# Attention and SwiGLU on one core: two VectorE casts one slot later, and V of batch 2 issued earlier in chunk 0

## The chip, the cores and the metric

The kernel runs on 1 core of one Trainium2 chip. The metric is the device time of one execution in microseconds (us). Engines are named as in the profile: PE is TensorE, DVE is VectorE, ACT is ScalarE, POOL is GpSimd, SP is SyncE.

## The reference

An attention with a learned decay for 8 batches, 8 heads, 576 positions and a head size of 64, followed by a feed-forward layer over 4608 tokens of width 512 with an inner width of 1536:

```python
def _attn_ref(q, k, v, s):
    scores = scale * np.matmul(q, k.transpose(0, 1, 3, 2))
    cum = np.cumsum(np.maximum(s, 0.0), axis=-1)
    bias = -(cum[:, :, :, None] - cum[:, :, None, :])
    scores = np.where(causal, -1000000000.0, scores + np.minimum(bias, 0.0))
    ...  # softmax over the last axis
    return np.matmul(attn, v)

def _moe_ref(x, w_gate, w_val, w_out, rms_g):
    xn = x / np.sqrt(np.mean(x * x, axis=-1, keepdims=True) + 1e-06) * rms_g
    g = xn @ w_gate
    silu = g * (1.0 / (1.0 + np.exp(-g)))
    return silu * (xn @ w_val) @ w_out
```

## The kernel before

**Stages.** A prologue does most of batch 0's attention. Then nine chunks of 512 tokens go through the feed-forward layer (`ffn`, line 660), and the attention of the later batches is threaded between their matmuls. A chunk has 12 blocks `fb` of the inner width: four matmuls give the gate (line 670, a bank of the PSUM ring `psF` of four), ACT takes a tanh of it into `T` (673), four more matmuls give the value (679, another bank of `psF`), DVE forms `U` from `T` and the gate's bank (682) and, one block later, `Ht` from `U` and the value's bank (675). Then come four output groups `tb` of 12 matmuls with `wout_sb` (692), whose results ACT copies (697) and SP stores.

**Slots.** Between the groups of matmuls `step` (line 599) is called, 36 times a chunk; each call is one slot, and the number of the slot in the chunk is its phase. In chunk 0 slot 2fb+1 follows the gate of block fb and slot 2fb+2 its value; slots 25 to 36 lie in the output groups, three to a group. A slot first emits what the slot before it left over (`pending`: the second half of the exponentials and the causal mask of a score step), then the scaling of finished attention rows, at most one entry of each side queue (`act_side`, `v_side`, `pool_side`, `dve_side`), and then a score step, an attention-times-V step or a transposition. An entry of a side queue is a pair of a condition and an action, and only the head of a queue is looked at. `later(queue, lag, fns)` gives a condition of a number of slots from now; `early` does too, and also asks for a phase below 24. The engines execute what is emitted for them strictly in that order: an instruction that waits holds all that is behind it on its engine.

**Batch 1's Q and K** are loaded by SP in the prologue as 32-bit numbers into `kq32` and cast to bf16 into `kqn` (`cast`, line 135): K's four full row groups by ACT and POOL, Q's groups 0 and 1 by DVE in slots 3 and 4 (the line that the diff changes), groups 2 and 3 by POOL in slots 3 and 4. PE then transposes `kqn` (line 184, into `psT` or a bank of `psF`), and ACT or DVE copies the result to `kqT` (190, 192). Behind the casts in `dve_side` stands `check(0, (0,))`: three instructions on batch 0's K (`check_mag`, line 369, and two `check_max`, 375), one in each odd slot.

**V** of a batch is loaded in five DMAs issued by POOL (`load_v`, line 173; the instruction is at 175), each casting to bf16 on the way, through `v_side`, one in an odd slot. After the last attention step of batch 0, in slot 10, `after_av` queues V of batch 2 with a lag of 16. `step` leaves the V queue and the POOL queue alone in slots 30 to 33 of chunk 0 and the V queue also from slot 34 on. So two of batch 2's V loads are issued in slots 27 and 29 of chunk 0 and three in chunk 1.

**Batch 2's Q and K** are loaded by ACT from slot 14 on; POOL casts Q in slots 24 to 28 (149, and 141 for the last rows) and K from slot 34 on (141).

**Attention rows** of a block (b, qb) of 128 positions: after the second half of the heads ACT or DVE sums the squares (321, 325), POOL forms the factor `al_all` in two instructions (328, 331), DVE scales the rows into `xs_sb` (338), and they get into `xnT` by a transposing DMA of SP (348) or, for batch 0 and block (1,3), by PE (357) and a copy. Chunk 1 needs batch 1's rows up to and including block (1,3); (1,3) is transposed by PE in slot 34 of chunk 0, between two output groups.

Of the kernel before, what the change touches and what calls it, by code (L numbers as in the profile page):

```python
# [26 lines left out]
def kernel(  # L27
# [107 lines left out]
    def cast(eng, b, w, r0, r1, h0=0, h1=H):  # L135
        o = kqn[:, b % 2, w, r0:r1, h0:h1, :]
        i = kq32[:, w].rearrange("p h (r d) -> p r h d", d=D)[:, r0:r1, h0:h1, :]
        if eng is nc.scalar:
            eng.activation(out=o, in_=i, func=AF.Copy)
        else:  # L140
            eng.tensor_copy(out=o, in_=i)  # L141
# [17 lines left out]
    def kq_dma(b, w, c):  # L159

        if w == 0:
            n = rows(c)
            src = kqn[0:n, b % 2, 0, c].rearrange("p h d -> p (h d)")
            dst = kqTx[:, b % 2, 0, c, :, 0:n]
        elif c < 4:
            src = kqn[32 * c:32 * c + 32, b % 2, w, 0:4].rearrange("p r h d -> p (r h d)")
            dst = kqTx[:, b % 2, w, c].rearrange("d h (r p) -> d (h r) p", r=4)
        else:
            src = kqn[0:64, b % 2, w, 4].rearrange("p h d -> p (h d)")
            dst = kqTx[:, b % 2, w, 4, :, 0:64]  # L170
        nc.sync.dma_start_transpose(out=dst, in_=src)

    def load_v(b, c):
        n = rows(c)
        nc.gpsimd.dma_start(  # L175
            out=v_sb[0:n, b % 2, c, :, 0:64],
            in_=v[b, :, c * 128:c * 128 + n, :].rearrange("h p d -> p h d"))
# [157 lines left out]
    def x_scale(b, qb):  # L335
        n = rows(qb)
        col = b * NSC + qb
        nc.vector.scalar_tensor_tensor(  # L338
            out=xs_sb[0:n, (b * NSC + qb) % NX, :], in0=x_sb[0:n, (b * NSC + qb) % NX, :],
            scalar=al_all[0:n, col:col + 1], in1=g_row[0:n], op0=ALU.mult, op1=ALU.mult)  # L340

    def xt_dma(b, qb):

        n = rows(qb)
        t0 = (b * S + qb * 128) % RING
        m = min(n, RING - t0)
        i = (b * NSC + qb) % NX
        nc.sync.dma_start_transpose(out=xnT[:, :, t0:t0 + m], in_=xs_sb[0:m, i, :])
        if m < n:
            nc.sync.dma_start_transpose(out=xnT[:, :, 0:n - m], in_=xs_sb[m:n, i, :])  # L350
# [30 lines left out]
    slot = [0]  # L381
    first, chunk = [0], [0]
# [11 lines left out]
    pool_side, dve_side, v_side, act_side = [], [], [], []  # L394
# [5 lines left out]
    def ready(lag, *key):  # L400
        return at(*key) + lag <= slot[0]

    def run_side(queue):
        if queue and queue[0][0]():
            queue.pop(0)[1]()
            return True
        return False

    def later(queue, lag, fns):
        t = slot[0] + lag  # L410
        queue.extend((lambda: slot[0] >= t, f) for f in fns)
# [17 lines left out]
    def phase():  # L429

        return slot[0] - first[0]
# [14 lines left out]
    def casts(b):  # L446

        def key(c):  # L450
            load_k(b, c)
            done["K", b, c] = slot[0]
            if c == NSC - 1:
                check(b)

        def over(w):
            done["cast", b, w] = slot[0]
            if b + 1 < B and (w == 1 or b + 1 < KB):
                loads(b + 1, w, early, 4)
            if w == 1:  # L460
                x_seq.extend((b, ww, c) for c in range(NSC) for ww in ((1, 0) if b >= KB else (1,)))
            else:
                done["cast", b] = slot[0]
                check(b)

        def free(w):
            return ready(0, "check", b - 2, w) and (
                ready(0, "T", b - 2) if w == 0 and b < KB + 2 else
                b < XB + 2 or ready(4, "X", b - 2, w, 4))
        if b >= KB:  # L470
            pool_side.extend((lambda: free(0) and slot[0] % 2 == 0, lambda c=c: key(c)) for c in range(NSC))
        fns = [(1, lambda r=r: cast_x(nc.gpsimd, b, 1, r)) for r in range(NSC)]
        fns += [(1, lambda: over(1))]
        if b < KB:
            fns += [(0, lambda r=r: cast(nc.gpsimd, b, 0, r, r + 1)) for r in range(NSC)]
            fns += [(0, lambda: over(0))]
        pool_side.extend((lambda w=w: ready(7, "raw", b, w) and free(w), f) for w, f in fns)
# [4 lines left out]

    def after_av(b):
        if b + 2 < B:
            (early if b else later)(v_side, 6 if b else 16, [
                lambda r=r: load_v(b + 2, r) for r in range(NSC)]
                + [lambda: done.__setitem__(("V", b + 2), slot[0])])

# [15 lines left out]
    def do_s(key, pair=None):  # L504
        b, kb, g = key
        second = s_step(b, kb, g, pair)
        done["S", b, kb, g] = slot[0]
        if kb == 4:
            done["S", b, 4, 1] = slot[0]
        last["S"] = slot[0]  # L510
        return second
# [12 lines left out]
    def do_xt(key, pX=None):  # L524
        b, qb = key
        xt_step(b, qb, pX)
        done["XT", b, qb] = slot[0]
        last["T"] = slot[0]
# [13 lines left out]
    def can_s():  # L542
        if not s_seq or not slot_free():
            return False
        b, kb, g = s_seq[0]
        if b == 1 and (phase() < 24 and phase() % 2 == 0 or kb == 4 and at("AV", 1, 3, 1) > slot[0]):
            return False
        due = SLOTS * ((b * S + kb * 128) // DM) - (26 if b == 1 else 18 if b < 4 else 14)
        if slot[0] - last["S"] < (4 if slot[0] < due - 24 else 3 if slot[0] < due else 2):
            return False  # L550
        if b >= XB:
            return all(ready(5, "X", b, 1, c) for c in (kb, min(kb + 1, 4))) and (
                ready(5, "X", b, 0, kb) if b >= KB else ready(3, "T", b) if kb >= 3 else
                all(ready(3, "T", b, hp, 0) for hp in (2 * g, 2 * g + 1)))
        if kb >= 3 and not ready(3, "T", b):
            return False
        if kb == 4:
            return True
        return all(ready(3, "T", b, 2 * g + j, w) for j in (0, 1) for w in (0, 1))
# [18 lines left out]
    def by_pe(b, qb):  # L578

        return b == 0 or (b, qb) == (1, 3)  # L580
# [18 lines left out]
    def step(bare=False):  # L599

        slot[0] += 1
        while pending:
            pending.pop(0)()
        moved = False
        if scaled[0] < len(x_list):
            b, qb = x_list[scaled[0]]
            if ready(3, "AV", b, qb, 1):
                x_scale(b, qb)
                scaled[0] += 1
                if not by_pe(b, qb):  # L610
                    assert xt_seq[0] == (b, qb)
                    xt_dma(*xt_seq.pop(0))
                    done["XT", b, qb] = slot[0] + 4
                    moved = True
        run_side(act_side)

        if not moved and x_seq and slot[0] - last["X"] >= 2 and not (
                scaled[0] < len(x_list) and ready(1, "AV", *x_list[scaled[0]], 1)):
            b, w, c = x_seq[0]
            if (ready(2, "cast", b, 1) and ready(1, "S", b - 2, 4, 0)  # L620
                    and (w == 1 or ready(7, "K", b, c))):
                x_seq.pop(0)
                kq_dma(b, w, c)
                done["X", b, w, c] = last["X"] = slot[0]
                if b >= KB and (w, c) == (0, NSC - 1) and b + 2 < B:
                    casts(b + 2)
        bare = bare or chunk[0] == 0 and 30 <= phase() <= 33
        if slot[0] % 2 and not bare and not (chunk[0] == 0 and phase() >= 34):
            run_side(v_side)
        if not bare:  # L630
            run_side(pool_side)
        run_side(dve_side)
        if can_s():
            pending.append(do_s(s_seq.pop(0)))
            if t_seq and t_seq[0][0] == 1 and can_t():
                do_t(t_seq.pop(0))
            return
        n = 0
        if can_xt():
            do_xt(xt_seq.pop(0))  # L640
            n += 1
        if can_av():
            do_av(av_seq.pop(0))
            n += 1
        if n < 2 and t_seq and can_t():
            do_t(t_seq.pop(0))
# [133 lines left out]
    with tc.manual_schedule():  # L780
# [26 lines left out]
        ACT, DVE, POOL = nc.scalar, nc.vector, nc.gpsimd  # L807
# [89 lines left out]
        def done_cast(w):  # L897
# [4 lines left out]
            lambda: (cast(POOL, 1, 0, 2, 3), cast(POOL, 1, 0, 3, 4)),  # L902
            lambda: (cast(POOL, 1, 1, 2, 3), done_cast(0)),
            lambda: cast(POOL, 1, 1, 3, 4), lambda: done_cast(1), lambda: cast(POOL, 1, 1, 4, 5)])
        later(dve_side, 3, [lambda r=r: cast(DVE, 1, 1, r, r + 1) for r in (0, 1)])
        later(v_side, 0, [
            lambda: load_v(1, 0), lambda: load_v(1, 1), lambda: load_v(1, 2),
            lambda: nc.gpsimd.dma_start(out=wout_sb,
# [204 lines left out]
```

## Time and profile before

| | us |
|---|---|
| median of 3 runs | 373.54 |
| runs | 373.54, 372.38, 373.56 |
| the profiled execution | 373.4 |
| its span, first to last instruction | 371.5 |
| PE busy in it | 346.3 (93%) |
| chunk 0's first gate matmul | 30.83 |
| chunk 1's first gate matmul | 74.53 |

The span is the time from the first to the last instruction on the core; 1.9 us of the execution's time lie outside it. A row of a view in order of time gives start, duration, engine, line, operation, output and inputs, count, and in brackets how long the engine stood idle before it and what ended that. Rows of consecutive instructions of one kind are merged into one with their count. The ends of matmuls are modelled, so rows of PE overlap at their edges.

### The profile page before, as it was taken

The numbers are of one execution on the slowest core, as the hardware profiler recorded it, in microseconds if no ns is written. First come the engines' busy times: TensorE is split into PE (matmuls) and PEld (weight loads), VectorE is DVE, ScalarE is ACT, GpSimd is POOL, SyncE is SP. The second block draws the span as 40 slices with busy tenths as digits, with TensorE's granted clock in tenths as the row PEclk, the third lists the DMA queues.
The fourth block names the chain that finished last, engine by engine and source line by source line (L and its number), as shares of the span: only waits on it lengthen the run. The fifth ranks groups of instructions, "written<-read, shape, count | busy, mean of one in ns | idle before, by whom it ended". The sixth has DMA issues, their size and how long they took to land.

```text
span 371.5 us, 6891 instructions
## 1 busy us (share of the span) xinstructions
PE 346.3 (93%) x2312; PEld 162.7 (44%) x2356; DVE 277.1 (75%) x523; ACT 238.7 (64%) x624; POOL 176.4 (47%) x281
## 2 busy tenths in 40 slices
PE   1888999899999999899999999999999999999992
PEld 1553444354444444444444444444444444444441
DVE  6777989499887878788889888885488558827820
ACT  3977687457977597777768776776777644223311
POOL 5968625966757474778837934533222300000000
PEclk9999999999999999999999999999999999999998
DMA  7999999999949499959969974993300230020011
GB/s 231 169 229 233 178 230 193 155 210 209 182 113 120 44 210 126 175 61 212 149 167 206 157 105 118 112 103 53 106 16 15 44 106 3 0 85 30 0 61 62
DMA packets 125627, 46.23 MB, mean 124 GB/s; under 512 B 104912, under 2 KB 120784, under 8 KB 125584
## 3 DMA queue, kind: packets, MB, share of 16 engines
q0 software_dynamic: 59920, 11.80, 42.9%
q1 hardware_dynamic: 53040, 24.33, 32.5%
q10 hardware_dynamic: 12624, 9.59, 10.4%
q8 instruction: 20, 0.33, 0.4%
q14 instruction: 23, 0.19, 0.2%
HBM read 38.16 MB, written 9.44 MB: 128 GB/s over the span
## 4 chain that ended last, share of the span: by engine, by line
PE 61%; DVE 14%; POOL 8%; issue 6%; DMA 5%; ACT 4%; ACTq 0%; POOLq 0%; DVEq 0%
PE psF L692 19%; PE psF L670 17%; PE psF L679 17%; PE psS L250 3%; DVE U L682 3%; DMA kq<-in_q_dram 3%; DVE Ht L675 2%; DVE x_sb L315 2%; POOL v_sb L175 2%; DVE xs_sb L338 2%; ACT E L274 2%; DVE acc L375 2%; POOL E L283 2%; DMA kq<-in_k_dram 1%; POOL kqn L141 1%
## 5 line engine op out<-in xcount | busy, mean ns | idle before, releaser
L274 ACT ACTIVATE E<-psS,biasK 128x256 bf16<-128x256 f32 (+3 forms) x352 | 115.1, 416 | 19.1 <-PE psS L250 18.0
L670 PE MATMUL psF<-xnT,wg_sb 128*128 128x512 bf16 x426 | 110.3, 379 | 2.6 <-DVE Ht L675 0.9
L679 PE MATMUL psF<-xnT,wv_sb 128*128 128x512 bf16 x408 | 109.3, 380 | 1.4
L692 PE MATMUL psF<-wout_sb,Ht 128*128 128x512 bf16 x419 | 100.5, 379 | 0.5 <-issue 0.2
L682 DVE SCALAR_TENSOR_TENSOR U<-T,psF 128x512 bf16<-128x512 f32 x108 | 73.7, 682 | 29.2 <-ACT T L673 29.0
L283 POOL TENSOR_SCALAR_AFFINE_SELECT E<-E 128x512 bf16<-128x512 bf16 x72 | 51.5, 716 | 85.5 <-ACT E L274 85.1
L673 ACT ACTIVATE T<-psF 128x512 f32<-128x512 f32 x108 | 64.6, 598 | 42.8 <-PE psF L670 37.5
L675 DVE TENSOR_TENSOR Ht<-U,psF 128x512 bf16<-128x512 bf16 x99 | 67.7, 683 | 6.6
L670 PEld LDWEIGHTS <-wg_sb 128*128 128x128 bf16 x432 | 38.8, 98 | 47.1 <-issue 8.0
L679 PEld LDWEIGHTS <-wv_sb 128*128 128x128 bf16 x432 | 38.6, 98 | 42.6 <-issue 4.6
L692 PEld LDWEIGHTS <-Ht 128*128 128x128 bf16 x432 | 38.7, 98 | 42.0 <-issue 2.3
L338 DVE SCALAR_TENSOR_TENSOR xs_sb<-x_sb,al_all,g_row 128x512 bf16<-128x512 bf16 (+1 forms) x40 | 31.9, 800 | 16.4 <-POOL al_all L331 14.8
L697 ACT ACTIVATE osb<-psF 128x512 f32<-128x512 f32 x36 | 21.4, 595 | 33.5 <-PE psF L692 30.5
L321 ACT ACTIVATE xs_sb<-x_sb 128x512 bf16<-128x512 bf16 (+1 forms) x36 | 23.0, 641 | 22.3 <-DVE x_sb L315 22.0
L175 POOL DMA_DIRECT2D v_sb<-in_v_dram x40 | 35.5, 888 | 0.3 <-issue 0.2
L375 DVE TENSOR_TENSOR acc<-acc,mag 128x1280 bf16<-128x1280 bf16 x32 | 29.0, 922 | 0.4
L250 PE MATMUL psS<-kqT 64*128 64x256 bf16 (+2 forms) x304 | 26.8, 262 | 1.7 <-ACT E L274 1.1
L306 PEld LDWEIGHTS <-E 128*128 128x128 bf16 x320 | 23.1, 101 | 11.3 <-POOL E L283 0.8
L328 POOL TENSOR_SCALAR al_all<-ss_all 128x1 f32<-128x1 f32 (+1 forms) x40 | 11.1, 278 | 29.8 <-ACT xs_sb L321 24.0
L300 PEld LDWEIGHTS <-E 128*128 128x128 bf16 x256 | 21.2, 101 | 8.1 <-DVE x_sb L315 0.7
L331 POOL TENSOR_TENSOR al_all<-al_all,mhalf 128x1 f32<-128x1 f32 (+1 forms) x40 | 22.3, 557 | 3.3
L141 POOL CAST kqn<-kq 128x512 bf16<-128x512 f32 (+1 forms) x30 | 20.7, 710 | 5.8 <-DMA kq<-in_k_dram 3.7
(94 smaller groups left out, 271.9 us busy)
## 6 DMA issues: line engine op xcount, KB each, us to landing
out_dram<-osb SPq DMA_DIRECT2D x36, 256.0 KB, 2.2
kq<-in_q_dram ACTq DMA_DIRECT2D x6, 1024.0 KB, 6.7
v_sb<-in_v_dram POOLq DMA_DIRECT2D x32, 128.0 KB, 6.0
kq<-in_k_dram ACTq DMA_DIRECT2D x2, 1024.0 KB, 9.3
kqn<-in_k_dram POOLq DMA_DIRECT2D x16, 128.0 KB, 4.8
wg_sb<-in_moe_w_gate_dram POOLq DMA_DIRECT2D x2, 768.0 KB, 10.1
wv_sb<-in_moe_w_val_dram POOLq DMA_DIRECT2D x2, 768.0 KB, 12.5
wout_sb<-in_moe_w_out_dram POOLq DMA_DIRECT2D x1, 1536.0 KB, 14.7
```

Source lines behind the costliest of these rows:

```text
L175: nc.gpsimd.dma_start(out=v_sb[0:n, b % 2, c, :, 0:64], in_=v[b, :, c * 128:c * 128 + n, :].rearrange("h p d -> p h d"))
L250: nc.tensor.matmul(pair[par][:, j * W:j * W + M], lhsT=kT, rhs=qT, start=(j == 0), stop=(j == nj - 1))
L274: nc.scalar.activation(out=eo, in_=ei, func=AF.Exp, scale=0.125, bias=biasK[:, kb, bh:bh + 1])
L283: nc.gpsimd.affine_select(out=Ev[:, :, 0:nq], in_=Ev[:, :, 0:nq], pattern=[[0, nh], [1, nq]], compare_op=ALU.is_ge, fill=0.0, base=0, chan ...
L338: nc.vector.scalar_tensor_tensor(out=xs_sb[0:n, (b * NSC + qb) % NX, :], in0=x_sb[0:n, (b * NSC + qb) % NX, :], scalar=al_all[0:n, col:col ...
L375: nc.vector.tensor_tensor(out=acc[:, sl], in0=acc[:, sl], in1=mag[:, sl], op=ALU.max)
L670: nc.tensor.matmul(Gp, lhsT=wg_sb[:, cc, fs], rhs=xnT[:, cc, x0:x0 + DM], start=(cc == 0), stop=(cc == CC - 1))
L673: nc.scalar.activation(out=T, in_=Gp, func=AF.Tanh, scale=0.5)
L675: nc.vector.tensor_tensor(out=Ht[:, fb - 1, :], in0=pend[0], in1=pend[1], op=ALU.mult)
L679: nc.tensor.matmul(Vp, lhsT=wv_sb[:, cc, fs], rhs=xnT[:, cc, x0:x0 + DM], start=(cc == 0), stop=(cc == CC - 1))
L682: nc.vector.scalar_tensor_tensor(out=U, in0=T, scalar=1.0, in1=Gp, op0=ALU.add, op1=ALU.mult)
L692: nc.tensor.matmul(Op, lhsT=Ht[:, fb, tb * 128:(tb + 1) * 128], rhs=wout_sb[:, fb, :], start=(fb == 0), stop=(fb == FB - 1))
```

## The change

The lag of the entry for DVE's two casts of batch 1's Q goes from 3 to 4 slots. The lag of batch 2's V goes from 16 to 10, and the phase from which chunk 0 issues no V goes from 34 to 24, so that its first two loads come in slots 21 and 23 and the other three, as before, in chunk 1. The entries behind the casts in `dve_side` move with them: the check of batch 0's K from slots 5, 7 and 9 to 7, 9 and 11.

```diff
     def after_av(b):
         if b + 2 < B:
-            (early if b else later)(v_side, 6 if b else 16, [
+            (early if b else later)(v_side, 6 if b else 10, [
                 lambda r=r: load_v(b + 2, r) for r in range(NSC)]
                 + [lambda: done.__setitem__(("V", b + 2), slot[0])])
...
-        if slot[0] % 2 and not bare and not (chunk[0] == 0 and phase() >= 34):
+        if slot[0] % 2 and not bare and not (chunk[0] == 0 and phase() >= 24):
             run_side(v_side)
...
-        later(dve_side, 3, [lambda r=r: cast(DVE, 1, 1, r, r + 1) for r in (0, 1)])
+        later(dve_side, 4, [lambda r=r: cast(DVE, 1, 1, r, r + 1) for r in (0, 1)])
```

## The prediction

> **What bounds the kernel now.** I read the page's busy shares first, then busy time by stretches, then the chain of waits, then single engines' rows in order of time around the places where the change acts.
>
> ```profile
> span 371.5 us, 6891 instructions
> PE 346.3 (93%) x2312; PEld 162.7 (44%) x2356; DVE 277.1 (75%) x523; ACT 238.7 (64%) x624; POOL 176.4 (47%) x281
> ```
>
> TensorE (PE) is busy for 93% of the span: a change pays only where it takes away one of the few stretches in which PE stands still, and any microsecond that PE gets back early moves all that is queued behind it. The busy time by stretches (columns: stretch, its length, then busy time and instruction count of each engine) finds two of them in chunk 0, which ends with the last of these stretches:
>
> ```profile
> 36.00:42.00 6.00, 4.98 (x41) 2.79 (x41) 5.86 (x11) 3.56 (x7) 5.01 (x6) 1.00 1.32 201
> 42.00:48.00 6.00, 5.95 (x53) 3.12 (x53) 5.93 (x13) 4.61 (x12) 3.05 (x6) 1.00 1.53 163
> ...
> 66.00:74.50 8.50, 6.93 (x54) 3.31 (x54) 3.48 (x7) 3.98 (x14) 8.16 (x14) 1.00 0.90 141
> ```
>
> From 36 to 42 us PE is idle for 6.00 - 4.98 = 1.02 us while VectorE (DVE, third) is full. From 66 to 74.5 us PE is idle for 8.50 - 6.93 = 1.57 us while GpSimd (POOL, fifth) is full. Between, at 42 to 48, PE has nothing to gain. The first edit acts in the first place, the V edits in the second.
>
> **Edit 1, DVE's two casts of batch 1's Q one slot later.** They stood at slots 3 and 4 and go to 4 and 5. DVE, ACT, PE and POOL in order of time (start, duration, idle time before in brackets):
>
> ```profile
> 35.39 0.43 DVE L141 CAST kqn<-kq 128x512 bf16<-128x512 f32 x1 [1.39 <-DMA kq<-in_q_dram]
> 35.73 0.68 DVE L682 SCALAR_TENSOR_TENSOR U<-T,psF 128x512 bf16<-128x512 f32 x1
> 36.33 0.85 DVE L141 CAST kqn<-kq 128x512 bf16<-128x512 f32 x1
> 37.11 0.67 DVE L675 TENSOR_TENSOR Ht<-U,psF 128x512 bf16<-128x512 bf16 x1
> ```
> ```profile
> 33.62 0.60 ACT L673 ACTIVATE T<-psF 128x512 f32<-128x512 f32 x1
> ```
> ```profile
> 37.83 1.02 PE L670 MATMUL psF<-xnT,wg_sb 128*128 128x512 bf16 x4 [0.88 <-DVE Ht L675]
> 38.69 0.39 PE L184 MATMUL psT<-ident_bf,kqn 128*128 128x128 bf16 x4
> ```
> ```profile
> 36.86 0.79 POOL L141 CAST kqn<-kq 128x512 bf16<-128x512 f32 x1
> ```
>
> The cast of slot 3 stands on DVE ahead of the gate product U of block 1 (L682), and waits 1.39 us for the 1 MB transfer of Q, which lands at 35.39. U's input T was ready at 33.62 + 0.60 = 34.22, so U is held 35.73 - 34.22 = 1.51 us by a cast that it doesn't need. Behind U stand the second cast and Ht of block 1 (L675), and it is this Ht that PE waits for, 0.88 us, before it may fill that psF bank with block 3's gate.
>
> With the casts one slot later DVE's order is U, cast, Ht, cast. U runs in the idle time before the transfer lands (34.2 to 34.9); the first cast still starts at 35.39; Ht follows it at 35.39 + 0.43 = 35.8 and ends by 36.5 in place of 37.11 + 0.67 = 37.78. PE comes to that point at 37.83 - 0.88 = 36.95, so the 0.88 us goes whole. What is late next: the transposition of Q at 38.69 reads all four casts. One PE group (38.69 - 37.83 = 0.86) after 36.95 is 37.81; GpSimd's own cast ends at 36.86 + 0.79 = 37.65, and DVE's second cast, now behind Ht, starts at 36.4 and ends by 37.3 at its slower price of 0.85. So both are just in time, and no new wait is larger than 0.1 us.
>
> DVE stays full afterwards, so what does it allow PE to keep? Its total work until 45 us is the same, but one U (0.60 from start to start, 36.33 - 35.73) has left the queue behind the transfer.
>
> ```profile
> 45.50 0.68 DVE L190 COPY kqT<-psT 128x512 bf16<-128x512 bf16 x1
> ```
>
> This copy out of psT, in slot 12, comes 0.6 us earlier, at 44.9. The lower bound of the edit is thus 0.60 us (DVE's gain), the upper bound 1.02 (all of PE's idle time in the stretch). Since 42 to 48 us shows no PE wait although DVE was late all through it, PE's needs there have slack, and I take 1.0, near the upper end. The three check instructions of batch 0's K move two slots later (to 7, 9 and 11), as one queue runs one entry a slot; they take the place of nothing on PE and cost nothing while that slack holds; if it is gone, up to the difference of the bounds, 0.4.
>
> The two casts differ: 0.43 where DVE started first, 0.85 beside a GpSimd instruction. The Trainium skill, SBUF — State Buffer, section "Who interferes with whom", says that a VectorE cast in a two-port mode and a GpSimd instruction shut each other out for the whole instruction, and the one that starts first wins; the 0.85 agrees. By that rule the second cast, still next to GpSimd's cast at 36.86, makes one of the two end about 0.4 later (an estimate from that page's rule and the rows), and the edit would be worth 0.6.
>
> **Edit 2, V of batch 2 at slots 21 and 23, none after slot 24 of chunk 0.** Before, two of the five loads were issued at slots 27 and 29. The chain of waits in order of time (start, length):
>
> ```profile
> 66.28 0.90 POOL v_sb L175
> ...
> 68.72 0.56 POOL al_all L331
> 69.28 0.91 POOL v_sb L175
> ...
> 70.53 0.58 POOL al_all L331
> 71.14 1.15 DVE xs_sb L338
> ...
> 72.33 0.40 PE psT L357 x4
> ```
>
> PE waits for the scaled rows of block (1,3), which need their factor al_all, and that stands on POOL behind both V loads, 0.90 + 0.91 = 1.81 us of issuing. Three rows say how much of this comes back:
>
> ```profile
> 68.28 0.19 ACT L321 ACTIVATION_READ_ACCUMULATOR xs_sb<-x_sb 128x1 f32 x1
> ```
> ```profile
> 69.32 0.75 DVE L338 SCALAR_TENSOR_TENSOR xs_sb<-x_sb,al_all,g_row 128x512 bf16<-128x512 bf16 x1 [1.60 <-ACT E L274]
> ```
> ```profile
> 68.05 2.76 PE L692 MATMUL psF<-wout_sb,Ht 128*128 128x512 bf16 x12
> ```
>
> The sum of squares of (1,3) is ready at 68.28 + 0.19 = 68.47. POOL's chain may move up by 1.81, from 70.53 + 0.58 = 71.11 to 69.3; the input allows the same to within 0.1. The scaling takes 0.75 (row at 69.32) instead of 1.15 (beside GpSimd's casts of K), so it ends at about 70.1, before PE comes free at 68.05 + 2.76 = 70.81. The wait of 72.33 - 70.81 = 1.52 us then goes whole, with 0.7 to spare. With edit 1's 1.0 us PE, DVE, ACT and POOL are all earlier alike, and the spare stays.
>
> At their new place the loads cost POOL the same 1.81 us:
>
> ```profile
> 57.88 0.56 POOL L331 TENSOR_TENSOR al_all<-al_all,mhalf 128x1 f32<-128x1 f32 x1
> 58.79 0.64 POOL L283 TENSOR_SCALAR_AFFINE_SELECT E<-E 128x512 bf16<-128x512 bf16 x1 [0.34 <-ACT E L274]
> 61.19 0.64 POOL L283 TENSOR_SCALAR_AFFINE_SELECT E<-E 128x512 bf16<-128x512 bf16 x1 [1.77 <-ACT E L274]
> 61.78 0.61 POOL L149 CAST kqn<-kq 128x512 bf16<-128x512 f32 x1
> 63.29 0.19 POOL L328 TENSOR_SCALAR al_all<-ss_all 128x1 f32<-128x1 f32 x1 [0.90 <-DVE rZ L313]
> ```
>
> POOL is free for 0.34 us before 58.79, 1.77 before 61.19 and 0.90 before 63.29, 3.01 in all. The load of slot 21 starts at 58.4 and pushes the mask of 58.79 to 59.3; that of slot 23 runs from about 60.0 to 60.9, before the mask of 61.19. So it costs nothing downstream. If that cover were gone, at most the 1.81 would come back to the last third.
>
> What is late next there is block (1,2)'s transfer into xnT, which chunk 1's first matmul needs. Its issue, its time to landing and the matmul:
>
> ```profile
> 70.09 1.19 SPq L348 DMA_TRANSPOSE xnT<-xs_sb  x1
> ```
> ```profile
> xnT<-xs_sb SPq DMA_TRANSPOSE x1, 3.4
> ```
> ```profile
> 74.53 1.03 PE L670 MATMUL psF<-xnT,wg_sb 128*128 128x512 bf16 x4
> ```
>
> It lands at 70.09 + 3.4 = 73.5, 1.0 us before it is used. It moves up only by one load, 0.9, and the matmul by 1.52, so 0.4 us of slack is left; the slack falls but isn't used up.
>
> **Sum.** 1.0 + 1.52 = 2.5 us. The profiled execution took 373.4 us, 1.9 around its span of 371.5; it becomes 370.9. The median of the three runs shown, 373.54, is 0.14 above it: 371.0. After 74.5 us nothing of the change is left but the earlier start, the remaining three V loads keep their slots, and PE is the bound, so I let the gain stand to the end. By the skill's rule for the casts it would be 371.4.
>
> **Rivals.** *One of the two waits stays.* Edit 1: DVE's full queue puts the wait back elsewhere, and only 1.5 comes: 372.0. For it speaks DVE at 5.86 and 5.93 of 6.00 us; against it, PE's full 5.95 beside the second. Edit 2: block (1,2)'s transfer takes its place at chunk 1's start because it lands later than 3.4, and only 1.0 comes: 372.5. For it speaks the 0.4 us of slack; against it, that the V loads' own traffic has left that stretch.
>
> *Nothing comes*, since a later wait on something that does not move (a transfer) takes both back: 373.5. Against it: 93% busy PE, and the loads behind chunk 0 are issued from the queues that move.
>
> *Slower.* The queue of GpSimd's transfers is long at the new place, and an issue may hold POOL until what is ahead of it has landed:
>
> ```profile
> v_sb<-in_v_dram POOLq DMA_DIRECT2D x1, 64.0 KB, 15.6
> ```
> ```profile
> 45.85 0.74 POOL L175 DMA_DIRECT2D v_sb<-in_v_dram  x1
> ```
> ```profile
> v_sb<-in_v_dram POOLq DMA_DIRECT2D x1, 128.0 KB, 3.7
> ```
>
> The last V load of batch 1, issued at 45.85, lands at 61.5. Were slot 21's load held until then and slot 23's until that one has landed, 3.7 later and 0.9 for its issue, POOL would be at 66.1, then a mask (0.64) and a cast (0.61), and the factor of 63.29 would come at 67.4: 4.1 late, less 1.81, is 2.3 lost on the chain that PE waits for: 375.8. It decides from the point at which that factor comes after 63.29 + 1.81 = 65.1. Against it: the issue at 45.85 took 0.74 with the queue as full.
>
> *The change does not do what it says*: the loads miss slots 21 and 23 and go to chunk 1. They are off the last third all the same: 371.0 too.
>
> **How the numbers follow.** Full gain 0.60 (its own range 370.2 to 371.6, from 0.6 to 1.02 for edit 1 and half a microsecond of changed overlaps either way); one wait stays 0.20, of it 0.12 at 372.0 and 0.08 at 372.5; nothing comes 0.08; slower 0.10; misses its slots 0.02. Measurement tells about 0.3%, 1.1 us: faster means below 372.4. Faster 0.60 + 0.12 + 0.02 = 0.74, same 0.08 + 0.08 = 0.16, slower 0.10. The range 370.2 to 372.6 takes in the first two cases and leaves out less than 2 in 10.
>
> **What would show it.** Right: U of block 1 starts near 34.2 before a cast that still waits for Q's transfer; no 0.88 before block 3's gate; two V loads on POOL between 58 and 61 us and none between 64 and 70; no wait of PE for the scaled rows at the end of chunk 0; chunk 1's first gate near 72.0 instead of 74.53. Wrong: a transposition of Q that waits for a cast, PE idle at 42 to 48 us, a V issue of several microseconds, or chunk 1 starting early and the last instruction not.

## The result, and the profile after

| kernel | median, us | runs | against the kernel before |
|---|---|---|---|
| before | 373.35 | 6 (372.38 to 373.56) | |
| changed | 370.10 | 6 (369.39 to 371.13) | ratio 0.9925, 95% interval 0.9909 to 0.9942 |
| changed, second comparison | 369.89 | 6 (369.16 to 370.59) | 0.9900 (0.9868 to 0.9932), before 373.01 |
| changed, third comparison | 370.85 | 6 (370.21 to 371.36) | 0.9937 (0.9918 to 0.9956), before 373.11 |

The change makes the kernel faster by 3.25, 3.12 and 2.26 us in three comparisons. The profiled execution of the changed kernel took 371.13 us, the longest of its six. Its page's head, and the stretches of chunk 0 that were read above for the kernel before:

```profile
span 369.5 us, 6891 instructions
PE 346.3 (94%) x2312; PEld 162.7 (44%) x2356; DVE 277.1 (75%) x523; ACT 238.4 (64%) x624; POOL 176.1 (48%) x281
```
```profile
36.00:42.00 6.00, 5.90 (x56) 3.52 (x56) 5.86 (x11) 4.26 (x8) 3.99 (x6) 1.00 1.46 198
42.00:48.00 6.00, 5.95 (x45) 2.88 (x44) 5.93 (x13) 4.87 (x12) 4.58 (x6) 1.00 1.28 136
66.00:72.15 6.15, 6.10 (x52) 2.98 (x52) 2.54 (x5) 3.44 (x12) 5.34 (x11) 1.00 0.75 187
```

PE does the same 346.3 us of work in a span 2.0 us shorter. Of the first stretch it now stands idle for 0.10 us in place of 1.02, and of the last one, up to chunk 1's first gate at 72.15, for 0.05 in place of 1.57. The rows in order of time at edit 1's place (DVE, then PE):

```profile
34.32 0.69 DVE L682 SCALAR_TENSOR_TENSOR U<-T,psF 128x512 bf16<-128x512 f32 x1 [0.25 <-ACT T L673]
35.81 0.43 DVE L141 CAST kqn<-kq 128x512 bf16<-128x512 f32 x1 [0.80 <-DMA kq<-in_q_dram]
36.16 0.68 DVE L675 TENSOR_TENSOR Ht<-U,psF 128x512 bf16<-128x512 bf16 x1
36.75 0.85 DVE L141 CAST kqn<-kq 128x512 bf16<-128x512 f32 x1
```
```profile
36.89 1.02 PE L670 MATMUL psF<-xnT,wg_sb 128*128 128x512 bf16 x4
37.75 0.60 PE L184 MATMUL psT<-ident_bf,kqn 128*128 128x128 bf16 x4
38.25 1.02 PE L679 MATMUL psF<-xnT,wv_sb 128*128 128x512 bf16 x4
```

U of block 1 goes ahead of the cast that waits for Q, Ht follows it, and block 3's gate has no wait. And at edit 2's places (POOL at the new place and in the last third, then DVE and PE at the end of chunk 0):

```profile
57.69 0.95 POOL L175 DMA_DIRECT2D v_sb<-in_v_dram  x1
58.65 0.65 POOL L283 TENSOR_SCALAR_AFFINE_SELECT E<-E 128x512 bf16<-128x512 bf16 x1
59.23 0.90 POOL L175 DMA_DIRECT2D v_sb<-in_v_dram  x1
60.48 0.63 POOL L283 TENSOR_SCALAR_AFFINE_SELECT E<-E 128x512 bf16<-128x512 bf16 x1 [0.36 <-ACT E L274]
...
67.09 0.55 POOL L331 TENSOR_TENSOR al_all<-al_all,mhalf 128x1 f32<-128x1 f32 x1
67.84 0.64 POOL L328 TENSOR_SCALAR al_all<-ss_all 128x1 f32<-128x1 f32 x1 [0.20 <-ACT xs_sb L321]
68.56 0.55 POOL L331 TENSOR_TENSOR al_all<-al_all,mhalf 128x1 f32<-128x1 f32 x1
```
```profile
67.67 0.75 DVE L338 SCALAR_TENSOR_TENSOR xs_sb<-x_sb,al_all,g_row 128x512 bf16<-128x512 bf16 x1 [0.68 <-POOL al_all L331]
69.14 0.75 DVE L338 SCALAR_TENSOR_TENSOR xs_sb<-x_sb,al_all,g_row 128x512 bf16<-128x512 bf16 x1 [0.71 <-POOL al_all L331]
```
```profile
69.95 0.40 PE L357 MATMUL psT<-ident_bf,xs_sb 128*128 128x128 bf16 x4
```

The two V loads stand in POOL's idle time around the masks, and the transposition of block (1,3), which waited 1.52 us, waits for nothing.

### The profile page after: what moved, and what is told of

The parts are those of the page before. It is cut to its first block, busy times and chain, and to the rows that moved or that the text cites. A ratio compares the mean times of both kernels' runs of the same rounds, so it can differ in the third digit from the quotient of the medians.

```text
span 369.5 us, 6891 instructions
## 1 busy us (share of the span) xinstructions
PE 346.3 (94%) x2312; PEld 162.7 (44%) x2356; DVE 277.1 (75%) x523; ACT 238.4 (64%) x624; POOL 176.1 (48%) x281
## 4 chain that ended last, share of the span: by engine, by line
PE 69%; DVE 9%; POOL 7%; issue 5%; DMA 5%; ACT 4%; ACTq 0%; SPq 0%; POOLq 0%; DVEq 0%
PE psF L692 22%; PE psF L670 19%; PE psF L679 19%; PE psS L250 4%; DMA kq<-in_q_dram 3%; ACT E L274 2%; POOL v_sb L175 2%; DVE acc L375 2%; DVE U L682 2%; DVE Ht L675 2%; POOL E L283 2%; DMA kq<-in_k_dram 2%; DVE x_sb L315 1%; POOL kqn L141 1%; PE psT L306 1%
## 5 line engine op out<-in xcount | busy, mean ns | idle before, releaser
L673 ACT ACTIVATE T<-psF 128x512 f32<-128x512 f32 x108 | 64.5, 597 | 42.1 <-PE psF L670 36.7
L338 DVE SCALAR_TENSOR_TENSOR xs_sb<-x_sb,al_all,g_row 128x512 bf16<-128x512 bf16 (+1 forms) x40 | 32.1, 804 | 15.0 <-POOL al_all L331 15.0
L375 DVE TENSOR_TENSOR acc<-acc,mag 128x1280 bf16<-128x1280 bf16 x32 | 29.0, 921 | 0.4
L328 POOL TENSOR_SCALAR al_all<-ss_all 128x1 f32<-128x1 f32 (+1 forms) x40 | 12.6, 316 | 28.2 <-ACT xs_sb L321 23.7
L250 PEld LDWEIGHTS <-kqT 64*128 64x128 bf16 x320 | 10.4, 97 | 30.5 <-issue 29.2
```

The lines of the kernel that those rows point to most:

```text
L250: nc.tensor.matmul(pair[par][:, j * W:j * W + M], lhsT=kT, rhs=qT, start=(j == 0), stop=(j == nj - 1))
L338: nc.vector.scalar_tensor_tensor(out=xs_sb[0:n, (b * NSC + qb) % NX, :], in0=x_sb[0:n, (b * NSC + qb) % NX, :], scalar=al_all[0:n, col:col ...
L375: nc.vector.tensor_tensor(out=acc[:, sl], in0=acc[:, sl], in1=mag[:, sl], op=ALU.max)
L673: nc.scalar.activation(out=T, in_=Gp, func=AF.Tanh, scale=0.5)
```

## The experiments

Chunk 0 is where the kernels differ, so each run is read by the same marks, in us after its own first gate matmul: DVE's first cast of Q and what held it (Q's transfer; the check of batch 0's Q, which is explained below; or neither, so that it ran straight behind U), the first output group, the transposition of (1,3), chunk 1's first gate; and last the length of chunks 2 and 3 together.

| kernel | first cast, held by | output group | (1,3) | chunk 1 | chunks 2+3 |
|---|---|---|---|---|---|
| before | 4.56, Q | 29.51 | 41.50 | 43.70 | 77.91 |
| before again | 4.49, check | 29.78 | 41.76 | 43.96 | 77.89 |
| changed | 4.90, Q | 28.71 | 39.04 | 41.24 | 78.33 |
| changed again | 5.09, check | 28.87 | 39.20 | 41.40 | 78.38 |
| changed, third | 4.28, Q | 28.58 | 38.90 | 41.10 | 78.34 |
| casts only | 4.02, neither | 28.11 | 40.08 | 42.28 | 78.36 |
| V only | 4.18, Q | 29.12 | 39.45 | 41.65 | 78.38 |
| V at 13 and 15 | 5.09, check | 28.88 | 39.19 | 41.38 | 78.34 |
| one V at 27 | 5.09, check | 28.88 | 40.49 | 42.70 | 78.23 |
| weights later | 4.02, neither | 28.10 | 38.42 | 40.62 | 78.34 |
| weights later again | 4.02, neither | 28.10 | 38.43 | 40.63 | 78.38 |
| cast at slot 26 | 4.02, neither | 28.11 | 38.46 | 40.66 | 77.90 |

**Each half of the change alone, the whole again, and V earlier still** (one chip, 21 runs of the kernel before).

Casts only:

```diff
-        later(dve_side, 3, [lambda r=r: cast(DVE, 1, 1, r, r + 1) for r in (0, 1)])
+        later(dve_side, 4, [lambda r=r: cast(DVE, 1, 1, r, r + 1) for r in (0, 1)])
```

> Edit 1 alone: DVE's casts at slots 4 and 5, V of batch 2 at slots 27 and 29 as before. Theory (two separate waits, each taken away by its own edit): no 0.88 us before block 3's gate, the 1.5 us of PE before the transposition of block (1,3) stays, chunk 1's first gate 0.8 us earlier after chunk 0's first gate than before (42.9 instead of 43.70 us), the execution 0.8 us below the kernel before. Rival 1 (POOL's queue sets the end of chunk 0 by itself): the wait at the end grows by what the first gives, chunk 1 starts as before, no difference. Rival 2 (most of the 3.2 us between the medians is this edit's, by changed overlaps behind chunk 0): 2 us or more below.

V only:

```diff
-            (early if b else later)(v_side, 6 if b else 16, [
+            (early if b else later)(v_side, 6 if b else 10, [
...
-        if slot[0] % 2 and not bare and not (chunk[0] == 0 and phase() >= 34):
+        if slot[0] % 2 and not bare and not (chunk[0] == 0 and phase() >= 24):
```

> Edit 2 alone: V of batch 2 at slots 21 and 23, the casts at slots 3 and 4 as before. Theory: the 0.88 us before block 3's gate stays, the 1.5 us before the transposition of block (1,3) goes, chunk 1's first gate 42.1 us after chunk 0's first (43.70 before), the execution 1.5 us below the kernel before. Rival 1 (the two edits help each other: without edit 1 POOL is later by 0.8 us at slots 21 to 23 and the loads push the masks): under 1 us below. Rival 2 (V's traffic beside batch 2's K load costs later): chunk 1 starts 1.6 us earlier and the end comes less than 0.8 us earlier.

The changed kernel again, without an edit:

> The changed kernel again, on the same chip as the others. Theory: chunk 1's first gate 41.2 us after chunk 0's first, the execution 2.4 us below the kernel before, that is the sum of the two edits alone, with some tenths of scatter from chunks 3 and 4. Rival: 3.2 us below, as the two medians stood, so that something behind chunk 0 is faster too.

On the changed kernel, V's lag 2 and its last phase 16, so that the loads come at slots 13 and 15:

```diff
-            (early if b else later)(v_side, 6 if b else 10, [
+            (early if b else later)(v_side, 6 if b else 2, [
...
-        if slot[0] % 2 and not bare and not (chunk[0] == 0 and phase() >= 24):
+        if slot[0] % 2 and not bare and not (chunk[0] == 0 and phase() >= 16):
```

> The changed kernel with the first two V loads at slots 13 and 15 in place of 21 and 23 (lag 2, no V from phase 16 on), when GpSimd's queue of transfers is fullest (the last V load of batch 1 landed at 61.5 us). Theory (only leaving the last third counts, an issue is not held by the transfers ahead of it): issues of 0.9 us each, the same time as the changed kernel within 0.3 us. Rival (an issue waits for what is ahead in its queue): issues of several microseconds between 46 and 61 us, masks of batch 1 late, 2 us or more above the changed kernel.

Casts only took 371.62 us (ratio 0.9958, 0.9939 to 0.9976), V only 371.60 (0.9952, 0.9927 to 0.9977), both together 369.89 (0.9900, 0.9868 to 0.9932), V at 13 and 15 370.55 (0.9916, 0.9885 to 0.9948). The two edits bring about the same, 0.4 to 0.5%, and by the medians, 1.39 and 1.41 us alone and 3.12 together, they add up within the intervals. Several expectations missed in size. With the casts alone chunk 1 started after 42.28 us and not 42.9, with V alone after 41.65 and not 42.1, because Q landed earlier than in the first profile before. The changed kernel again, expected 2.4 us below the kernel before, came out 3.12 below, nearer to its rival's 3.2; but its profile shows nothing faster behind chunk 0, as the section on the 0.45 us shows. V at 13 and 15 lies 0.66 above it and not within 0.3, with intervals that overlap. PE's row at the end of chunk 0 with the casts alone, and the rows of DVE and PE at edit 1's place with V alone:

```profile
71.04 0.40 PE L357 MATMUL psT<-ident_bf,xs_sb 128*128 128x128 bf16 x4 [1.50 <-DVE xs_sb L338]
```
```profile
35.02 0.43 DVE L141 CAST kqn<-kq 128x512 bf16<-128x512 f32 x1 [1.01 <-DMA kq<-in_q_dram]
35.36 0.68 DVE L682 SCALAR_TENSOR_TENSOR U<-T,psF 128x512 bf16<-128x512 f32 x1
```
```profile
38.79 1.02 PE L679 MATMUL psF<-xnT,wv_sb 128*128 128x512 bf16 x4 [0.51 <-DVE U L682]
```

Each edit takes away its own wait and leaves the other's: 1.50 us stays without edit 2, and without edit 1 the cast still holds U, and PE waits 0.51 for a later U in place of 0.88 for Ht. With V at slots 13 and 15 the loads are issued while batch 1's last V load, issued at 46.21, is still under way; it lands 11.9 us later:

```profile
47.55 0.90 POOL L175 DMA_DIRECT2D v_sb<-in_v_dram  x1
48.47 0.65 POOL L283 TENSOR_SCALAR_AFFINE_SELECT E<-E 128x512 bf16<-128x512 bf16 x1
49.06 0.89 POOL L175 DMA_DIRECT2D v_sb<-in_v_dram  x1
```

An issue takes 0.9 us there too, and chunk 0 has the length of the changed kernel's: so a long queue does not hold an issue here, which was the mechanism of the slower rival. From the output group to the transposition of (1,3) it takes 11.97 to 11.99 us with both loads in the last third (before, before again, casts only) and 10.31 to 10.35 with none: edit 2 is worth 1.65 us.

**One V load in the last third, and the check of batch 0's K later** (on the changed kernel):

```diff
-            (early if b else later)(v_side, 6 if b else 10, [
+            (early if b else later)(v_side, 6 if b else 16, [
...
-        if slot[0] % 2 and not bare and not (chunk[0] == 0 and phase() >= 24):
+        if slot[0] % 2 and not bare and not (chunk[0] == 0 and phase() >= 28):
```

> The changed kernel with one V load in the last third: lag 16 again and no V from phase 28 on, so the first load is issued in slot 27 and the other four in chunk 1. Theory (POOL's queue sets the end of chunk 0, and the changed kernel has hardly any spare left there: its scaling ended at 69.89 us, PE came to the transposition at 69.95): one issue of 0.9 us gives back most of it, PE waits 0.6 to 0.8 us before the transposition of block (1,3), from the first output group to it 11.0 us (10.33 without a load, 11.99 with two). Rival (the spare of 0.7 us that the prediction worked out): a wait of 0.2 us or none. The end of the run may differ by the one V load more in chunk 1.

```diff
-            return slot[0] % 2 and chunk[0] == b
+            return slot[0] % 2 and chunk[0] == b and (b or phase() >= 17)
```

> The changed kernel with the check of batch 0's K at slots 17, 19 and 21 instead of 7, 9 and 11, where VectorE has less to do. Theory (0.2 us of edit 1 is lost between the gates of blocks 6 and 7, because the last check instruction now stands in slot 11 ahead of what PE needs there): the gate of block 7 comes 11.5 us after Q's transfer has landed (11.7 in the changed kernel, 12.8 before), the execution 0.2 us lower, inside the scatter. Rival 1 (VectorE's load holds PE all along): 0.6 us or more lower. Rival 2 (at 17 to 21 the check delays the rows of batch 1): the same or higher.

With one V load: 372.46 us (0.9970, 0.9957 to 0.9983). PE's row, POOL's two behind the load at 65.78, and the scaling of (1,3) on DVE:

```profile
71.51 0.40 PE L357 MATMUL psT<-ident_bf,xs_sb 128*128 128x128 bf16 x4 [1.14 <-DVE xs_sb L338]
```
```profile
68.00 0.19 POOL L328 TENSOR_SCALAR al_all<-ss_all 128x1 f32<-128x1 f32 x1
...
68.91 0.75 POOL L328 TENSOR_SCALAR al_all<-ss_all 128x1 f32<-128x1 f32 x1
```
```profile
70.33 1.13 DVE L338 SCALAR_TENSOR_TENSOR xs_sb<-x_sb,al_all,g_row 128x512 bf16<-128x512 bf16 x1 [0.71 <-POOL al_all L331]
```

One load alone costs 11.61 - 10.33 = 1.28 us, the second only 0.37 more. The wait is 1.14 us where 0.6 to 0.8 was expected. Hardly anything is to spare at the end of chunk 0, so the load's delay counts: beside the changed kernel, at like marks, the factor L328 starts 0.79 later and takes 0.75 in place of 0.64. The rest, 0.38, comes in the scaling itself, 1.13 in place of 0.75, since it now runs beside POOL's mask and casts of K.

The late check: 372.44 us (0.9964, 0.9945 to 0.9983). Its rows stand on DVE at 54.70 and 58.45 between the sums of batch 1's rows, and PE waits again at the end of chunk 0, for the scaling, as the second rival of this run had it:

```profile
72.14 0.40 PE L357 MATMUL psT<-ident_bf,xs_sb 128*128 128x128 bf16 x4 [0.91 <-DVE xs_sb L338]
```

So the check's place matters there, and slots 7 to 11, where the change puts it, are the better one. This profile and that of the last run below aren't in the table, since PE's granted clock fell for some three microseconds at their start of chunk 0. They can be compared with each other: both come to the first output group after 29.8 us, and from there to the transposition it takes 11.39 us with the late check and 10.36 in the last run, with the check at 7 to 11. What the run was made for, a gain of 0.2 us between the gates of blocks 6 and 7, can't be read from it, as both profiles have 2.6 us there. By stretches, this kernel and then the changed one:

```profile
31.00:34.00 3.00, 3.00 (x8) 1.12 (x8) 1.79 (x3) 1.26 (x3) 3.00 (x5) 0.52 1.22 251
```
```profile
31.00:34.00 3.00, 2.95 (x20) 1.27 (x21) 2.40 (x4) 1.94 (x4) 2.37 (x5) 1.00 1.14 264
```

**The second halves of the weights later, and before again.** On the changed kernel the two loads leave the prologue for the first entry of the POOL queue, so that they go behind batch 1's Q in the transfers:

```diff
-        load_w(moe_w_gate, wg_sb, 1)
-        load_w(moe_w_val, wv_sb, 1)
...
-            lambda: cast(POOL, 1, 0, 4, 5),
+            lambda: (cast(POOL, 1, 0, 4, 5), load_w(moe_w_gate, wg_sb, 1), load_w(moe_w_val, wv_sb, 1)),
```

> The changed kernel with the second halves of the gate and value weights (two DMAs of POOL, 768 KB each) issued 3 us later, behind POOL's first cast of batch 1's K, so that Q's transfer has more of the DMA engines. Theory (what is left of the first wait hangs on the time at which Q's transfer lands, 4.9 to 5.1 us after chunk 0's first gate): Q lands at 4.0 or earlier, the first output group 28.1 us after the first gate (28.7 to 28.9 in the changed kernel), the execution 0.6 us lower. Rival (the weights are now late): PE waits for them at block 6, and the time is the same or higher by up to 2 us.

> The kernel before, a second profile. Theory: from Q's landing to the first output group 24.9 us again (25.0 and 24.9 in the two profiles with the casts at slots 3 and 4; 23.8 in those with the casts at 4 and 5), wherever Q lands; 1.5 us of wait before the transposition of (1,3); chunks 2 and 3 together 77.9 us as in its first profile (78.3 to 78.4 in all changed kernels), so that 0.4 us is given back there. Rival: 78.3 us in this profile, so that the first profile was a chance and nothing is given back.

> The kernel with the late weight loads of the run before, on one chip beside the changed kernel. Theory (what chunk 0 saves is kept to the end, less the same 0.45 us in chunk 3): Q lands about 4.0 us after the first gate, chunk 0 lasts 40.6 us against 41.2 to 41.4, and the time is 0.6 us below the changed kernel's median. Rival (the time is set elsewhere, or the earlier landing is part of the scatter of the transfers): chunk 0 within 0.2 us of the changed kernel's or the median within 0.2 us of it.

> The changed kernel once more, as the measure for the run with late weight loads. Both theories: 370.0 to 370.5 us median, 0.9 to 1.0 per cent below the kernel before; Q's landing between 4.9 and 5.1 us after the first gate and the first output group 23.8 us behind it. Were the landing 4.0 to 4.2, the landings would be scatter and not the kernel's doing.

The first took 370.43 us (0.9927, 0.9914 to 0.9939); beside the changed kernel on one chip it took 370.13 (0.9921, 0.9901 to 0.9940) and that 370.85 (0.9937, 0.9918 to 0.9956). Chunk 0 is 0.5 to 0.8 us shorter in both profiles and the second median 0.72 lower, as the theory has it. That the late loads are the cause isn't shown all the same: the last kernel of the table keeps the early loads, its chunk 0 is the changed kernel's, and it took 40.66 us too. Whether late loads make an early landing more frequent stays open. The kernel before, again, kept its 1.50 us of wait before the transposition and its 77.9 us for chunks 2 and 3, as expected; its output group came 25.3 us behind the cast and not 24.9, since the check held the cast and not Q. The third profile of the changed kernel missed its expectation as well (cast at 4.28 in place of 4.9, output group 24.3 behind it in place of 23.8). The profiles of one and the same chunk 0 thus differ by scatter, with two sources. One is the landing of Q. The other shows in DVE's rows just before and in the first stretch of chunk 0, here before again (with the casts on POOL), then before, then the casts on POOL in the changed kernel, third:

```profile
30.58 3.55 DVE L375 TENSOR_TENSOR acc<-acc,mag 128x1280 bf16<-128x1280 bf16 x2
34.06 0.68 DVE L682 SCALAR_TENSOR_TENSOR U<-T,psF 128x512 bf16<-128x512 f32 x1
```
```profile
31.72 1.73 POOL L141 CAST kqn<-kq 128x512 bf16<-128x512 f32 x3
```
```profile
30.46 1.56 DVE L375 TENSOR_TENSOR acc<-acc,mag 128x1280 bf16<-128x1280 bf16 x2
```
```profile
31.75 2.00 POOL L141 CAST kqn<-kq 128x512 bf16<-128x512 f32 x3
```

In four profiles ("check" in the table) the last instruction of the check of batch 0's Q took 2.81 us in place of 0.82, until POOL's three casts of K were through, and it is then DVE that comes late to the first cast, not Q. In the changed kernel, third, the two start as far apart (31.35 and 31.75 there, 31.33 and 31.72 before again), and there the check takes 0.82 and the casts 0.27 more.

**Where 0.45 us goes back.** Every changed kernel above takes 0.4 to 0.5 us longer for chunks 2 and 3 than the kernel before (one V at 27: 0.3). The rows in order of time: before (DVE, POOL), then the changed kernel, third (DVE, POOL, ACT, PE):

```profile
181.60 0.74 DVE L338 SCALAR_TENSOR_TENSOR xs_sb<-x_sb,al_all,g_row 128x512 bf16<-128x512 bf16 x1
```
```profile
180.57 2.24 POOL L149 CAST kqn<-kq 128x512 bf16<-128x512 f32 x3
```
```profile
179.07 1.24 DVE L338 SCALAR_TENSOR_TENSOR xs_sb<-x_sb,al_all,g_row 128x512 bf16<-128x512 bf16 x1
```
```profile
178.04 1.71 POOL L149 CAST kqn<-kq 128x512 bf16<-128x512 f32 x3
```
```profile
186.54 0.63 ACT L321 ACTIVATE xs_sb<-x_sb 128x512 bf16<-128x512 bf16 x1 [2.50 <-DVE x_sb L315]
```
```profile
189.25 0.40 PE L250 MATMUL psS<-kqT 64*128 64x256 bf16 x4 [0.58 <-ACT E L274]
```

In both kernels the scaling starts 1.03 us after the first of POOL's three casts, while the second one runs. Before, the scaling is short (0.74) and the casts take 0.53 longer; changed, the casts are short and the scaling takes 0.50 longer. Which of scaling and third cast went first is read from these lengths, since the starts are alike. DVE has no idle time behind it, so ACT's sum of squares, its exponentials and PE's score matmuls come late. In one experiment, one V at 27, the scaling took 0.74 again, and PE's wait was 0.15; it still took 78.23 us, since ACT's sum of squares ahead of that scaling waited 1.32 us for DVE, where it waits 0.98 in the kernel before. Why DVE is later there isn't followed further. To test what the third cast does to the scaling, one instruction of the changed kernel was moved, and then the same on the kernel with the late weights:

```diff
-        if not bare:
+        if not bare and not (chunk[0] == 3 and phase() == 25):
             run_side(pool_side)
```

> The changed kernel with one instruction elsewhere: in chunk 3 GpSimd's fourth cast of batch 6's Q comes at slot 26, behind the causal mask of that slot, and not at slot 25 ahead of it. Everything else keeps its order. Open is why every changed kernel takes 78.3 to 78.4 us for chunks 2 and 3, and the kernel before 77.9. Theory: DVE's scaling (L338, at 179.1 us in the changed kernel) and this cast become ready within some ten ns of each other; in the kernel before the scaling went first and took 0.74, in the changed kernel the cast goes first and the scaling takes 1.23; DVE is full behind it, and PE waits the difference, 0.58 us, at its score matmuls at 189.3. With the cast out of the way the scaling takes 0.75 or less, the 0.58 wait is below 0.2 and the two chunks take 77.8 to 78.0 us. Rival (the 0.58 comes from the earlier start itself, as ACT's and PE's order meets otherwise in chunk 3): the scaling gets short, but the wait stays at 0.5 to 0.6 and the two chunks at 78.3 to 78.4.

> The changed kernel with the late weight loads and with the same cast at slot 26 of chunk 3. Theory: chunk 0 takes 40.6 us, chunks 2 and 3 77.9, so 0.6 to 0.7 and 0.45 us less than the changed kernel: 369.3 to 369.6 us where that took 370.1 to 370.85, about 1.1 per cent below the kernel before. Rival (the 0.58 us wait stays): 369.9 to 370.4.

The rows of the first (DVE, POOL):

```profile
178.70 0.74 DVE L338 SCALAR_TENSOR_TENSOR xs_sb<-x_sb,al_all,g_row 128x512 bf16<-128x512 bf16 x1
```
```profile
177.68 1.16 POOL L149 CAST kqn<-kq 128x512 bf16<-128x512 f32 x2
179.09 0.85 POOL L283 TENSOR_SCALAR_AFFINE_SELECT E<-E 128x512 bf16<-128x512 bf16 x1 [0.26 <-ACT E L274]
```

The scaling is short, PE has no wait at the end of chunk 3, and the two chunks take 77.90 us: the cause is shown, in the trace. Its span is 368.6 us, its one time 370.51. With the late weights too the two chunks take 77.90, but the six runs have a median of 370.47 (0.9932, 0.9912 to 0.9953), where 369.3 to 369.6 was expected. Its profile, the longest of the six at 371.77, had PE's granted clock at 0.52 from 31 to 34 us again, and chunk 0 took 42.36. Six repeats of the changed kernel lie up to 1.7 us apart, ten of V only 2.1, so a gain of 0.45 us, seen in the trace, can't be told by these medians, and no version is shown to beat the changed kernel.

**What differs elsewhere.** Chunks 4 to 8, counted from 0 and each from its first gate to the next one's or to the last store, take the same time within some 0.02 us in every profile. The end scatters: the last store's issue in the changed kernel, and in the changed kernel again:

```profile
363.68 0.33 SPq L699 DMA_DIRECT2D out_dram<-osb  x1
```
```profile
363.67 0.33 SPq L699 DMA_DIRECT2D out_dram<-osb  x1
```

The spans end at 369.5 and 368.9, so 0.6 us of difference lies behind this issue; among all fourteen profiles it is 5.2 to 5.9 us from there to the end, with no order by kernel.

## Why the prediction was right, and where its steps were off

The direction and the cause held: two waits of PE in chunk 0, each taken away by its own edit, and the time, 370.10, 369.89 and 370.85, came out by the sum's 371.0 within 1.1 us, twice a little under the low end of 370.2. That the number is so near is in part luck: the sum of 2.5 us was reached in chunk 0, then 0.45 of it was lost again where the prediction let it stand, and the medians of two comparisons show more than the traces account for.

**Edit 1, 1.0 us between 0.60 and 1.02.** Right in mechanism and about in size; both the order U, cast, Ht, cast and the vanished 0.88 show. Among profiles held by the check, the output group comes at 29.78 with the old order and at 28.87 or 28.88 with the new: 0.90. Where Q holds the cast, the old order follows Q one to one (29.51 at 4.56, 29.12 at 4.18), which at the changed kernel's landings would be 29.85 and 29.22, against 28.71 and 28.58: 1.14 and 0.64. These estimates go past the prediction's upper bound of 1.02 at one end. The two first profiles show only 29.51 - 28.71 = 0.80, since Q landed 0.34 later in the second. That this landing is no constant the prediction didn't see. Of the skill's rule for the casts: the Trainium skill, SBUF — State Buffer, section "Who interferes with whom", says that a VectorE instruction in a two-port mode, as a cast can be, contends with GpSimd, and that the one that issues second is blocked for the whole instruction of the other. The trace agrees: the second cast took 0.85 again, and the transposition of Q behind it stretches to 0.60 from 0.39. PE comes from block 3's gate to its value in 1.36 us (36.89 to 38.25), where 1.09 are enough in the run with the casts alone: 0.27, less than the 0.4 that would have made 371.4, but more than the 0.1 that "just in time" had allowed. In the third profile, with Q earlier, it was nothing.

**The check "costs nothing".** Two thirds right. No PE wait comes of it, but in the changed kernel block 6's gate to block 7's gate takes 2.80 us where it took 2.60, behind a check now at 44.60 on DVE, ahead of the copy at 45.33 that the prediction had put at 44.9. It is so where the first cast comes late: in the table, 2.79 or 2.80 in the five profiles of the new order with that cast at 4.28 or later, and 2.60 in the four with it at 4.02, whose check stands in the same slots. Up to 0.4 had been allowed for.

**Edit 2, 1.52 us with 0.7 to spare.** The loads at slots 21 and 23 took 0.95 and 0.90, and ran where the prediction put them. The mask behind the first came 0.58 us later at like marks, 0.5 by the prediction, and no wait of PE came of it: the gates of blocks 10 and 11 are 2.40 us apart as before. The wait went whole, and the edit is worth 1.65. The spare failed: the scaling ended at 69.14 + 0.75 = 69.89, 0.06 before the transposition at 69.95. The step that failed is the factor's chain: L328 took 0.64 in place of 0.18, because at 67.84 it now meets the scaling of the block before it (67.67, 0.75). So one load left in the last third meets a spare of 0.06 and not 0.7, and it makes the scaling long as well: it costs 1.28 us and not 0.2.

**"The gain stands to the end".** This step failed, by 0.45 us, in chunk 3, at a tie between two instructions that the earlier start decided the other way. From the first gate to chunk 1's the changed kernel gains 2.5 to 2.6 us by like pairs (43.70 against 41.24 and 41.10, both held by Q; 43.96 against 41.40, both by the check). From the first gate to the last chunk's the same pairs (302.56 against 300.51 and 300.36, 302.80 against 300.72) keep 2.1 to 2.2. The medians gained 2.3 to 3.3. What they have above the traces isn't explained; the scatter of 0.6 us behind the last store is of that size, and single profiles can't settle it.

**The rivals.** Neither wait came back elsewhere, and the transfer of block (1,2) didn't take the place of the old wait: chunk 1's gate follows the transposition of (1,3) by 2.19 to 2.21 us in every kernel of the table. The slower rival fell with V at 13 and 15.

## What to carry to other kernels

An instruction that waits for a transfer belongs behind whatever is ready on its engine, and a DMA issue of 0.9 us belongs in its engine's idle time, not in the chain of the last rows; both show as a PE wait whose releaser was itself waiting. Check a "spare" by asking which short instruction on the freed chain now meets the other engine. And compare profiles at like marks (the same first cast, the same chunk) before reading a difference of half a microsecond: an early start carried through a static order can lose it again at a tie far behind.

## What the runs showed of the hardware

DVE and POOL shut each other out for whole instructions where both are near: a scaling took 0.74 or 1.24 us with its start, against POOL's casts, at 1.03 us in both cases. The Trainium skill, SBUF — State Buffer, section "Who interferes with whom", says that a VectorE instruction with two inputs in SBUF contends with a GpSimd instruction that reads it, and that the order of issue decides. The lengths at L338 and L375 agree that the two contend; the order the rows don't show, as the check starts 0.4 us ahead of POOL's casts both where it is short and where it is long. What surprised is the length: the check lost 2.0 us in one instruction, more than any one instruction of POOL took beside it, as it waited for all three casts (1.73 together). PE's granted clock fell to 0.52 for some 3 us at the start of chunk 0 in two of fourteen profiles, which made that chunk's second gate come 1.5 us later.
